# The last 64 keys of two pairs of heads as one unit of four 64x64 tiles, and a new order of all instructions

## The chip, the cores and the metric

One core of one Trainium2 chip runs the whole program. The metric is the device time of one execution in microseconds. The kernel before takes 428.75 us, the median of 3 runs (428.47 to 429.63).

## What is computed

Three layers follow each other: an attention with capped scores over 2 x 12 heads of 448 positions, a gated layer with a mixing matrix over positions (named `moe`), and a mixer layer (`moe2`). Cut to what matters:

```python
def _attn_ref(q, k, v, cap):                     # q, k, v: 2 x 12 x 448 x 64
    scores = q @ k.transpose(0, 1, 3, 2) / np.sqrt(64)
    scores = cap * np.tanh(scores / cap)
    attn = np.exp(scores - np.max(scores, axis=-1, keepdims=True))
    return attn / (np.sum(attn, axis=-1, keepdims=True) + 1e-09) @ v

def _moe_ref(x, w_in, g_ln, w_sg, b_sg, w_out):  # x: 2 x 448 x 768
    u, v = np.split(gelu_tanh(x @ w_in), 2, axis=-1)
    v_s = np.einsum('ts,bsd->btd', w_sg, layer_norm(v) * g_ln) + b_sg[None, :, None]
    return x + (u * v_s) @ w_out

def _moe2_ref(x, w_tok1, w_tok2, w_ch1, w_ch2):
    u = x + (np.maximum(x.transpose(0, 2, 1) @ w_tok1, 0.0) @ w_tok2).transpose(0, 2, 1)
    return u + np.maximum(u @ w_ch1, 0.0) @ w_ch2
```

## The kernel before

Two heads form a pair, 128 partitions wide; there are 12 pairs, 6 for each of the two batches. The 448 keys of a pair are cut into three chunks of 128 and a rest of 64. All matmuls of the attention are in float32, which the trace shows as two records a matmul.

- *Scores* (`scores`, line 578). For a chunk, each head's 64-row block of keys and queries makes one 64x128 tile of TensorE; the two heads run side by side by rows (mode `ROWS`) into a tile `sc` of two PSUM banks, [128 keys, head, 448 queries]. The rest (`last` in `attention_all`, line 692) is done for both heads at once with 128 rows and two column tiles (mode `COLS`); its keys are padded with zeros, and the result [64 keys of head 0 above 64 keys of head 1, 448] goes to one bank of the pool `gm`.
- *Weighing* (`weigh`, lines 554 and 562). ScalarE makes tanh and then exp of each score tile, 896 columns wide for a chunk, 448 for the rest.
- *Values* (`values`, line 591). Four units a pair, one for each chunk and one for the rest, two column tiles side by side (`COLS`), summed up in one bank.
- *Sums* (`sums`, lines 605 and 626). The sums of the weights are a matmul with ones. VectorE or GpSimd adds the chunks first. `LEVEL` says how many tiles are left to separate matmuls: 1 for the first six pairs (the rest has a unit of its own), 0 for the last six (the rest is added too, in two adds of half the partitions).
- *Normalising* (`normalise`): VectorE transposes the sums, takes the reciprocal, transposes back, multiplies the values' bank, and splits the result in a high and a low part for the dense layers.

The dense layers use three matmuls in a reduced float format for one exact one (`three`, line 314). While the second batch's pairs go through the attention, the first batch's seven units of the gated layer (three `v_unit`, four `u_unit`, 18 matmuls each) are put between them; their gelu (line 794) runs after the attention's exps, since it is in another function table of ScalarE. Weights arrive as pairs of 32-bit words and are rebuilt by ScalarE (lines 450, 461, 474) and VectorE.

The order of everything is made by a planner at build time (`Plan.schedule`). Every step is an operation with a duration, a key and buffers from pools of fixed size (`sc` 2, `gm` 4, `a` 21). The planner takes, engine by engine, the operation that can start first, ties by key, with a price for a change of TensorE's mode (`TURN`, `STAY`) and a latency from one engine to the next (`LAT`). The result is a fixed list for each engine, which runs it in that order and waits on semaphores.

## Time and profile before

| What | us |
|---|---|
| median of 3 runs | 428.75 |
| the profiled execution | 427.77 |
| its span, first to last instruction | 425.9 |
| TensorE busy | 415.3 |
| VectorE busy | 253.8 |
| ScalarE busy | 248.9 |

The span is what the trace covers; the profiled execution's own time is 1.87 us longer. PE is TensorE, PEld its weight loads, DVE VectorE, ACT ScalarE, POOL GpSimd. Line numbers are those of the listing above. The attention runs from about 4 to 136 us; its last sums unit starts at 134.96, and the dense stage alone follows from 136.02. The records of TensorE overlap, so the time that a step takes of the engine is the interval between starts.

### The profile page before, as it was taken

The page shows a single profiled execution, that of the slowest core. Times are in us where ns is not written, and L with a number is a line of the kernel's source. Part 1 is how long each engine was busy: PE and PEld are TensorE (multiplying, and loading weights), DVE is VectorE, ACT ScalarE, POOL GpSimd, SP SyncE. Part 2 cuts the span into 40 slices and gives each one's busy share as a digit, 9 for nine tenths or more (in the row PEclk, how much of TensorE's full clock was granted, in tenths as well). Part 3 has the DMA queues.
Part 4 walks back from the last instruction along what each step waited for, and adds up shares of the span by engine and source line. Part 5 has one row for each costly group of instructions (what it writes and reads, how often), then busy time and mean ns, then how long its engine had stood idle before and what let it go on. Part 6 is the DMA issues. An engine that isn't in the chain of part 4 may idle for free. (4 is left out here: it accounts for less than half of the span.)

```text
span 425.9 us, 5397 instructions
## 1 busy us (share of the span) xinstructions
PE 415.3 (98%) x2036; PEld 318.9 (75%) x2036; DVE 253.8 (60%) x407; ACT 248.9 (58%) x372; POOL 89.4 (21%) x88
## 2 busy tenths in 40 slices
PE   8999999999997999999999999999999999999995
PEld 4333335565644899999999989989898899899885
DVE  1859979798645875995556898666312241434211
ACT  6898899889796556426647826575604323444100
POOL 1113130202000321756005295101010010011010
PEclk9999999999998999999999999999999999999999
DMA  7855243442200003005303105544401315442201
GB/s 251 344 164 190 78 169 125 145 163 76 98 1 25 26 10 122 11 2 159 133 0 100 49 3 160 153 131 152 145 0 49 100 45 173 142 148 98 90 21 49
DMA packets 14867, 43.66 MB, mean 102 GB/s; under 512 B 1905, under 2 KB 3569, under 8 KB 14833
## 3 DMA queue, kind: packets, MB, share of 16 engines
q1 hardware_dynamic: 14688, 43.13, 31.2%
q8 instruction: 18, 0.29, 0.3%
q14 instruction: 17, 0.13, 0.1%
q10 hardware_dynamic: 144, 0.10, 0.1%
HBM read 40.47 MB, written 2.75 MB: 101 GB/s over the span
## 5 line engine op out<-in xcount | busy, mean ns | idle before, releaser
L314 PE MATMUL gm<-a,a 128*128 128x384 f32 (+2 forms) x556 | 112.9, 359 | 0.0
L314 PEld LDWEIGHTS gm<-a,a 128*128 128x128 f32 x556 | 100.6, 188 | 8.5
L314 PE MATMUL sc<-x,a 128*128 128x512 f32 (+1 forms) x432 | 87.3, 363 | 0.0
L314 PEld LDWEIGHTS sc<-x,a 128*128 128x128 f32 x432 | 78.3, 188 | 9.0
L481 DVE SCALAR_TENSOR_TENSOR t<-r,t 128x512 int32<-128x512 int32 (+1 forms) x52 | 41.1, 793 | 28.4 <-ACT t L474 27.8
L314 PE MATMUL gm<-q,a 128*128 128x448 f32 (+2 forms) x268 | 57.0, 366 | 0.0
L450 ACT ACTIVATE r<-r 128x512 f32<-128x512 f32 (+1 forms) x58 | 38.9, 670 | 29.2 <-DMA r<-ch_in 27.1
L461 ACT ACTIVATE t<-r 128x512 uint16<-128x512 uint16 (+1 forms) x52 | 40.8, 784 | 24.5 <-DVE a L418 24.2
L314 PEld LDWEIGHTS gm<-q,a 128*128 128x128 f32 x268 | 49.8, 188 | 4.9
L419 POOL TENSOR_TENSOR a<-t,a 128x512 fp32r<-128x512 f32 x17 | 25.8, 1519 | 95.6 <-DVE a L402 65.8
L474 ACT ACTIVATE t<-r 128x512 f16<-128x512 f32 (+1 forms) x52 | 40.3, 775 | 0.0
L418 DVE TENSOR_TENSOR a<-t,a 128x512 fp32r<-128x512 f32 x39 | 27.1, 698 | 20.3 <-POOL a L406 18.8
L406 POOL TENSOR_SCALAR a<-t 128x512 fp32r<-128x512 f32 x18 | 11.2, 619 | 126.7 <-PE gm L314 65.6
L605 DVE TENSOR_TENSOR a<-a,a 128x896 f32<-128x896 f32 x23 | 24.9, 1084 | 20.9 <-ACT a L562 20.8
L591 PE MATMUL gm<-a,v 128*64 128x448 f32 x144 | 33.7, 561 | 3.6 <-ACT a L562 3.6
L554 ACT ACTIVATE a<-sc,qs 128x896 f32<-128x896 f32 x36 | 34.8, 1001 | 3.0 <-PE sc L578 2.9
L562 ACT ACTIVATE a<-a,acap 128x896 f32<-128x896 f32 x36 | 36.2, 1042 | 0.0
L314 PEld LDWEIGHTS gm<-x,a 128*128 128x128 f32 x144 | 26.6, 188 | 6.0 <-issue 2.7
L314 PE MATMUL gm<-x,a 128*128 128x448 f32 x144 | 30.9, 370 | 0.0
L578 PE MATMUL sc<-q 64*128 64x448 f32 x132 | 29.8, 566 | 1.1 <-ACT a L554 0.7
L979 DVE SCALAR_TENSOR_TENSOR a<-sc,a 128x896 fp32r<-128x896 f32 x9 | 9.8, 1091 | 30.4 <-ACT a L976 30.4
L314 PE MATMUL gm<-a,x 128*128 128x512 f32 x108 | 27.2, 406 | 0.0
(102 smaller groups left out, 422.2 us busy)
## 6 DMA issues: line engine op xcount, KB each, us to landing
r<-ch_in SPq DMA_DIRECT2D x36, 512.0 KB, 3.7
r<-w_in_in SPq DMA_DIRECT2D x12, 512.0 KB, 4.8
q<-qk_in SPq DMA_DIRECT2D x11, 480.0 KB, 5.6
v<-va_in SPq DMA_DIRECT2D x12, 256.0 KB, 3.0
r<-w_out_in SPq DMA_DIRECT2D x6, 512.0 KB, 3.1
out_t<-h SPq DMA_DIRECT2D x6, 256.0 KB, 2.3
r<-tok_in SPq DMA_DIRECT2D x2, 512.0 KB, 3.3
out_t<-h SPq DMA_DIRECT2D x5, 192.0 KB, 3.9
```

Of the source, the lines that this page charges most:

```text
L314: self.nc.tensor.matmul(view(), l, rr, start=(i + m == 0), stop=(i + m == n - 1))
L418: "DVE": ("DVE", n / 0.96 + 155, lambda: nc.vector.tensor_tensor(**args()), not psum),
L419: "POOL": ("POOL", n * 2.3 + 60, lambda: nc.gpsimd.tensor_tensor(**args()), True),
L450: lambda: nc.scalar.activation(raw[:, :, 1].bitcast(F32), raw[:, :, 1].bitcast(F32), AF.Copy, scale=2.0**-112),
L461: lambda: nc.scalar.activation(t.ap.bitcast(U16)[:, 0::2], raw.ap.rearrange("p n t -> p (n t)").bitcast(U16)[:, 1::4], AF.Copy, scale=2.0* ...
L474: lambda: nc.scalar.activation(t.ap.bitcast(F16)[:, 1::2], raw[:, :, 1].bitcast(F32), AF.Copy),
L481: lambda: nc.vector.scalar_tensor_tensor(out=t.ap, in0=raw[:, :, 1], scalar=3, in1=t.ap, op0=ALU.logical_shift_left, op1=ALU.bitwise_or),
L554: lambda: nc.scalar.activation(te.ap, sc.ap.rearrange("p (n c) -> p n c", c=512)[:, 0:nn, :S] if nn == 1 else sc[:, 0:nn, :S], AF.Tanh, sc ...
L562: lambda: nc.scalar.activation(te.ap, te.ap, AF.Exp, scale=self.acap),
L578: nc.tensor.matmul(sc[:, h, :S], part(rows, ks), part(rows, QC), start=True, stop=True)
L591: nc.tensor.matmul(A[cols, :S], V[:, 2 * j + h], E[j][:, 0 if j == 3 else h], start=(j == 0), stop=(j == 2),)
L605: "DVE": ("DVE", n / 0.96 + 155, lambda: nc.vector.tensor_tensor(**args()), True),
```

## The change

The last 64 keys of an even pair and the odd pair after it become one unit. `scores_rest` writes one two-bank tile: the even pair's 64 keys in the lower 64 partitions, the odd pair's in the upper, head 0 in one bank and head 1 in the other, by four matmuls of 64 rows and 64 columns (mode `QUAD`). One tanh and one exp of 896 columns follow, and `values_rest` adds both pairs' parts by four 64x64 tiles to the two pairs' banks. The scores of a chunk are cut into 64x64 tiles too (`SPLIT`), four instead of two. `LEVEL` is 0 for all pairs, and the rest is added to a pair's sums in one add of 64 partitions and 896 columns. The zero padding of the keys is gone (`QKW` 960 to 896), and a pair's rest of v lies in the lower or upper partitions by turns.

The planner's durations are new: latency by engine, fixed costs of operations, a price for a change of ScalarE's table, a DMA issue of 420 ns instead of 60. A gelu now waits for all exps of the latest pair. So the order differs everywhere.

```diff
-LEVEL = (1,) * 6 + (0,) * 6
+LEVEL = (0,) * 12
...
-LAT = 140.0
-TURN, STAY = 110.0, 250.0
+LAT = {"PE": 225.0, "ACT": 160.0, "DVE": 140.0, "POOL": 140.0, "SP": 55.0}
+TURN, STAY = 200.0, 250.0
+TABLE = 1290.0
...
+                    if o.table and o.table != table:
+                        c = (max(t, near) + TABLE,) + c[1:3] + (max(t, clock[eng]) + TABLE, o, way)
...
-            ks = slice(KJ[j], KJ[j] + 128)
-            for h, rows in enumerate((LO, UP)):
-                nc.tensor.matmul(sc[:, h, :S], part(rows, ks), part(rows, QC), start=True, stop=True)
-
-        self.pe(3.7, fn, tiles if j else tiles[:1], [sc], key).mode = ROWS
+            for c0 in range(0, 128, 64) if SPLIT else (None,):
+                for h, rows in enumerate((LO, UP)):
+                    at = slice(0, 128) if c0 is None else slice(c0, c0 + 64)
+                    ks = slice(KJ[j] + at.start, KJ[j] + at.stop)
+                    nc.tensor.matmul(sc[at, h, :S], part(rows, ks), part(rows, QC), start=True, stop=True)
+
+        self.pe(3.7, fn, tiles if j else tiles[:1], [sc], key).mode = QUAD if SPLIT else ROWS
...
+    def scores_rest(self, qks, key):
...
+            for (part, _, _), cols in zip(qks, (LO, UP)):
+                for h, rows in enumerate((LO, UP)):
+                    nc.tensor.matmul(sc[cols, h, :S], part(rows, KR), part(rows, QC), start=True, stop=True)
...
+    def values_rest(self, qks, E, As, key):
...
+            for m, rows in enumerate((LO, UP)):
+                for h, cols in enumerate((LO, UP)):
+                    nc.tensor.matmul(As[m][cols, :S], qks[m][2][rows, 6 + h], E[rows, h], start=(m == 1), stop=(m == 0))
...
         if level < 1:
-            for h, rows in enumerate((LO, UP)):
-                f = lambda h=h, rows=rows: F[rows, h]
-                self.add(S, f, f, lambda rows=rows: E[3][rows, 0], [E[3], F], [F], key - 5, ON["F"])
+            rows = (LO, UP)[int(odd)]
+            f = lambda: F[rows]
+            self.add(2 * S, f, f, lambda: E[3][rows], [E[3], F], [F], key - 5, ON["F"])
...
-                self.pe(3.7, last, qk[1], [sc], k0 + 1.3).mode = COLS
-                self.weigh(sc, 1, E[3], k0 + 1.3)
+                if not odd:
+                    sc = self.scores_rest(qks, k0 + KQ)
+                    self.weigh(sc, 2, Q, k0 + KQ)
...
-                self.values(oqk, oE, oA[0], [3, 2], k0 + 2)
-                self.sums(oE, oA[1], k0 + 2.5, LEVEL[n - 1])
+                self.values(oqk, oE, oA[0], [2], k0 + 2, was)
+                if not was:
+                    self.values_rest(oqks, oE[3], oAs, k0 + 2.1)
+                self.sums(oE, oA[1], k0 + 2.5, LEVEL[n - 1], was)
...
-        if self.last_exp:
-
-            o.deps.append(self.last_exp)
+        if self.exps:
+            o.deps += self.exps[max(self.exps)]
```

Three places show what the new order does. A row is a line of the code, the operation, the tile it writes and those it reads, and its shape; `x2` to `x4` are equal instructions in a row. The number behind a tile's name only tells tiles apart. In the new code line 595 is `scores`, 608 `scores_rest`, 621 `values`, 638 `values_rest`, 667 the sums, 323 the dense matmuls, 566 and 575 tanh and exp, 834 gelu.

The first place is TensorE around the value unit of the third chunk of the seventh pair, whose weights are `a_526` before and `a_536` now, up to the first dense matmuls. Before:

```order
L578 MATMUL sc_513<-q_123 128x448 x2
L626 MATMUL gm_449<-a_429,ones 64x448 x2
L591 MATMUL gm_458<-a_493,v_323 64x448 x2
L626 MATMUL gm_497<-a_511,ones 64x448 x2
L591 MATMUL gm_539<-a_503,v_376 64x448 x2
L591 MATMUL gm_539<-a_522,v_376 64x448 x2
L692 MATMUL gm_553<-q_250 64x448 x2
L591 MATMUL gm_539<-h_483,v_376 64x448 x2
L591 MATMUL gm_539<-a_526,v_376 64x448 x2
L578 MATMUL sc_572<-q_250 128x448 x2
L578 MATMUL sc_582<-q_250 128x448 x2
L314 MATMUL gm_589<-a_193,x_230 128x512 x3
```

Now:

```order
L608 MATMUL sc_527<-q_210 64x448 x2
L595 MATMUL sc_542<-q_210 64x448 x4
L595 MATMUL sc_550<-q_210 64x448 x4
L667 MATMUL gm_558<-a_464,ones 64x448 x2
L621 MATMUL gm_562<-a_507,v_390 64x448 x2
L621 MATMUL gm_562<-a_516,v_390 64x448 x2
L621 MATMUL gm_562<-a_536,v_390 64x448 x2
L595 MATMUL sc_585<-q_210 64x448 x4
L595 MATMUL sc_594<-q_278 64x448 x4
L667 MATMUL gm_602<-a_547,ones 64x448 x2
L595 MATMUL sc_611<-q_278 64x448 x4
L323 MATMUL gm_619<-a_214,x_268 128x512 x3
```

Before, the rest of a pair has units of its own here (`L692`, scores of the eighth pair; `L591` with `h_483`, values of the seventh), and the dense matmuls (`L314`) begin three rows behind `a_526`. Now the two rows `L608` are the joint rest of both pairs (the second of them is shown), no value unit of a rest stands here, and the dense matmuls begin five rows behind `a_536`.

The second place is ScalarE at the end of the attention. Before:

```order
L554 ACTIVATE a_1045<-sc_1031,qs 128x896
L554 ACTIVATE a_1055<-sc_1039,qs 128x896
L562 ACT_TABLE_LOAD
L562 ACTIVATE a_1045<-a_1045,acap 128x896
L562 ACTIVATE a_1055<-a_1055,acap 128x896
L554 ACTIVATE a_1073<-sc_1061,qs 128x896
L794 ACT_TABLE_LOAD
L794 ACTIVATE h_964<-h_964 128x448
L562 ACT_TABLE_LOAD
L562 ACTIVATE a_1073<-a_1073,acap 128x896
L794 ACT_TABLE_LOAD
L794 ACTIVATE h_1007<-h_1007 128x448
```

Now:

```order
L566 ACTIVATE a_1071<-sc_1056,qs 128x896
L566 ACTIVATE a_1079<-sc_1063,qs 128x896
L575 ACTIVATE a_1071<-a_1071,acap 128x896
L575 ACTIVATE a_1079<-a_1079,acap 128x896
L566 ACTIVATE a_1106<-sc_1081,qs 128x896
L575 ACTIVATE a_1106<-a_1106,acap 128x896
L410 COPY h_1120<-gm_1090 128x448
L834 ACT_TABLE_LOAD
L834 ACTIVATE h_1127<-a_721 128x512
L834 ACTIVATE h_1134<-a_758 128x512
L834 ACTIVATE h_1137<-a_844 128x512
L834 ACTIVATE h_923<-h_923 128x448
```

Before, three table loads stand between tanh, exp and gelu of the last pair. Now the last exp (`a_1106`) comes first, then one table load, then the gelus in a row.

The third place is TensorE at the same time, up to the last sums (`gm_1114` before, `gm_1131` now). Before:

```order
L578 MATMUL sc_1061<-q_490 128x448 x2
L314 MATMUL gm_1048<-x_411,a_696 128x448 x3
L314 MATMUL gm_1048<-x_477,a_720 128x448 x3
L314 MATMUL gm_1048<-x_570,a_777 128x448 x3
L314 MATMUL gm_1048<-x_577,a_820 128x448 x3
L591 MATMUL gm_1085<-a_1045,v_880 64x448 x2
L591 MATMUL gm_1085<-a_1055,v_880 64x448 x2
L591 MATMUL gm_1085<-h_1019,v_880 64x448 x2
L591 MATMUL gm_1085<-a_1073,v_880 64x448 x2
L314 MATMUL gm_1103<-a_193,x_230 128x512 x3
L314 MATMUL gm_1103<-a_244,x_325 128x512 x3
L626 MATMUL gm_1114<-a_1075,ones 64x448 x2
```

Now:

```order
L595 MATMUL sc_1081<-q_462 64x448 x4
L323 MATMUL gm_1090<-x_268,a_654 128x448 x3
L323 MATMUL gm_1090<-x_362,a_691 128x448 x3
L323 MATMUL gm_1090<-x_423,a_748 128x448 x3
L323 MATMUL gm_1090<-x_511,a_771 128x448 x3
L323 MATMUL gm_1090<-x_609,a_834 128x448 x3
L323 MATMUL gm_1090<-x_674,a_864 128x448 x3
L621 MATMUL gm_1074<-a_1071,v_876 64x448 x2
L621 MATMUL gm_1074<-a_1079,v_876 64x448 x2
L621 MATMUL gm_1074<-a_1106,v_876 64x448 x2
L667 MATMUL gm_1131<-a_1108,ones 64x448 x2
L323 MATMUL gm_1139<-a_214,x_268 128x512 x3
```

Before, six dense matmuls of the next stage (`gm_1103`) stand ahead of the last sums, and a value unit of the rest (`h_1019`) among the last values. Now the whole dense unit `gm_1090` stands between the last scores and the last values, and the next stage (`gm_1139`) begins behind the sums.

## Rows read from the trace of the kernel before

**Rows 1.** The page's busy times: us (share of the span) and instructions of each engine.
```profile
PE 415.3 (98%) x2036; PEld 318.9 (75%) x2036; DVE 253.8 (60%) x407; ACT 248.9 (58%) x372; POOL 89.4 (21%) x88
```

**Rows 2.** Stretches: their us, then busy us of each engine, PEclk, DMA share, GB/s.
```profile
4.00:63.00 59.00, 57.39 (x276) 19.27 (x276) 43.93 (x79) 52.39 (x68) 12.68 (x8) 1.00 0.60 206
63.00:127.00 64.00, 63.61 (x300) 35.57 (x298) 49.96 (x90) 57.21 (x80) 7.04 (x7) 1.00 0.31 101
...
130.90:134.50 3.60, 3.60 (x9) 1.82 (x10) 2.42 (x4) 2.83 (x5) 0.00 (x0) 0.53 0.02 5
...
140.00:400.00 260.00, 260.00 (x1309) 235.98 (x1308) 147.87 (x217) 129.73 (x214) 66.03 (x60) 1.00 0.28 88
```

**Rows 3.** Timeline of TensorE: start us, us to the group's end, what, how many records.
```profile
76.04 4.42 PE L314 MATMUL gm<-a,x 128*128 128x512 f32 x18
80.38 1.77 PE L578 MATMUL sc<-q 64*128 64x448 f32 x8
...
102.34 0.92 PE L591 MATMUL gm<-a,v 128*64 128x448 f32 x4
103.09 0.92 PE L626 MATMUL gm<-a,ones 128*64 128x448 f32 x4
103.94 3.91 PE L314 MATMUL gm<-x,a 128*128 128x448 f32 x18
107.78 1.77 PE L578 MATMUL sc<-q 64*128 64x448 f32 x8
109.49 3.91 PE L314 MATMUL gm<-x,a 128*128 128x448 f32 x18
```

**Rows 4.** Timeline of TensorE at the attention's end.
```profile
130.88 1.71 PE L591 MATMUL gm<-a,v 128*64 128x448 f32 x4 [3.26 <-ACT a L562]
132.53 2.51 PE L314 MATMUL gm<-a,x 128*128 128x512 f32 x6
134.96 1.13 PE L626 MATMUL gm<-a,ones 128*64 128x448 f32 x4
136.02 11.17 PE L314 MATMUL gm<-a,x 128*128 128x512 f32 x48
```

**Rows 5.** Timeline of ScalarE at the attention's end.
```profile
128.50 1.28 ACT L562 ACT_TABLE_LOAD   x1
129.79 1.04 ACT L562 ACTIVATE a<-a,acap 128x896 f32<-128x896 f32 x1
```

**Rows 6.** Timeline of ScalarE in the attention's first part.
```profile
5.73 1.90 ACT L554 ACTIVATE a<-sc,qs 128x896 f32<-128x896 f32 x2 [0.18 <-DVE guard L357]
...
22.47 1.89 ACT L554 ACTIVATE a<-sc,qs 128x896 f32<-128x896 f32 x2
24.25 1.97 ACT L562 ACTIVATE a<-a,acap 128x896 f32<-128x896 f32 x2
26.11 1.90 ACT L554 ACTIVATE a<-sc,qs 128x896 f32<-128x896 f32 x2
...
29.76 0.69 ACT L450 ACTIVATE r<-r 128x512 f32<-128x512 f32 x1
30.34 0.99 ACT L554 ACTIVATE a<-sc,qs 128x896 f32<-128x896 f32 x1
```

**Rows 7.** Waits of ScalarE, 0 to 64 us: us in total, times, longest.
```profile
ACT h L554 <- PE gm L692: 3.7, 2, 2.0
...
ACT a L554 <- PE sc L578: 1.3, 1, 1.3
```

**Rows 8.** Timeline of TensorE at the attention's start.
```profile
3.90 1.39 PE L578 MATMUL sc<-a 64*128 64x448 f32 x4
...
8.29 1.02 PE L578 MATMUL sc<-q 64*128 64x448 f32 x4 [0.39 <-DMA q<-qk_in]
```

**Rows 9.** A group of VectorE on the page: busy us, mean ns, idle before.
```profile
L605 DVE TENSOR_TENSOR a<-a,a 128x896 f32<-128x896 f32 x23 | 24.9, 1084 | 20.9 <-ACT a L562 20.8
```

**Rows 10.** Timeline of TensorE's weight loads among column-tiled units.
```profile
100.08 0.14 PEld L591 LDWEIGHTS gm<-a,v 128*64 128x64 f32 x2 [0.23 <-issue]
```

More of the change, by code (lines that the diff above doesn't have):

```diff
@@ L109 @@
 class Op:
-    __slots__ = ("ways", "key", "seq", "deps", "bufs", "new", "eng", "fn", "start", "end", "nbytes", "nwait", "mode")
+    __slots__ = ("ways", "key", "seq", "deps", "bufs", "new", "eng", "fn", "start", "end", "nbytes", "nwait", "mode", "table")
 class Plan:
@@ L122, in op @@
         o.ways, o.key, o.seq, o.nbytes = ways, key, len(self.ops), nbytes
-        o.deps, o.new, o.mode = [], [], WHOLE
+        o.deps, o.new, o.mode, o.table = [], [], WHOLE, None
         o.bufs = list(dict.fromkeys(list(r) + list(w)))
@@ L180, in schedule @@
         mode = WHOLE
+        table = "exp"
         def earliest(o, way):
@@ L223, in schedule @@
                 mode = o.mode
+            table = o.table or table
             o.eng, dur, o.fn = way[:3]
@@ L241, in schedule @@
                 b.users -= 1
-                b.end = max(b.end, o.end)
+                b.end = max(b.end, o.end + LAT[o.eng])
                 if b.users == 0 and b.tag in free:
@@ L400, in cast @@
         made = {
-            "ACT": ("ACT", n / 1.2 + 180, lambda: nc.scalar.copy(out(), src()), False),
-            "DVE": ("DVE", n / 0.96 / (1 if psum else 2) + 155, lambda: nc.vector.tensor_copy(out(), src()), not psum),
+            "ACT": ("ACT", n / 1.2 + (60 if psum else 95), lambda: nc.scalar.copy(out(), src()), False),
+            "DVE": ("DVE", n / 0.96 / (1 if psum else 2) + 70, lambda: nc.vector.tensor_copy(out(), src()), not psum),
             "POOL": (
@@ L454, in weight @@
                 [raw],
+                130,
                 key=key,
@@ L553, in weigh @@
             nn * S,
-            lambda: nc.scalar.activation(te.ap, sc.ap.rearrange("p (n c) -> p n c", c=512)[:, 0:nn, :S] if nn == 1 else sc[:, 0:nn, :S], AF.Tanh, scale=self.qs),
+            lambda: nc.scalar.activation(te.ap, sc[:, 0:nn, :S], AF.Tanh, scale=self.qs),
             [sc, self.cb],
             [te],
-            60,
+            145,
             key,
+            "exp",
         )
-        self.last_exp = self.exps[int(key // 10)] = self.act(
+        e = self.act(
             nn * S,
@@ L564, in weigh @@
             [te],
-            190,
+            185,
             key + dt,
+            "exp",
         )
+        self.exps.setdefault(int(key // 10), []).append(e)
     def scores(self, qk, j, key):
@@ L593, in av, with fn @@
                         V[:, 2 * j + h],
-                        E[j][:, 0 if j == 3 else h],
-                        start=(j == 0),
-                        stop=(j == 2),
+                        E[j][:, h],
+                        start=(j == 0 and not odd),
+                        stop=(j == 2 and odd),
                     )
             self.pe(3.7, av, [V, E[j]], [A], key).mode = COLS
+    def values_rest(self, qks, E, As, key):
+        nc = self.nc
+        def fn():
+            for m, rows in enumerate((LO, UP)):
+                for h, cols in enumerate((LO, UP)):
+                    nc.tensor.matmul(As[m][cols, :S], qks[m][2][rows, 6 + h], E[rows, h], start=(m == 1), stop=(m == 0))
+        self.pe(3.7, fn, [qks[0][2], qks[1][2], E], As, key).mode = QUAD
     def add(self, n, out, a, b, r, w, key, on):
@@ L608, in add, with sums @@
         self.plan.op([made[e] + (t,) for e, t in on.items()], key, r, w)
-    def sums(self, E, A, key, level):
+    def sums(self, E, A, key, level, odd):
         nc = self.nc
@@ L676, in attention_all @@
             k0 = 10.0 * n
+            odd = n % 2 == 1
             if n < B * NP:
-                qk = self.pair_in(n)
+                if not odd:
+                    qks = [self.pair_in(n), self.pair_in(n + 1)]
+                    Q = self.a([128, 2, S])
+                    As = [self.bank(), self.bank()]
+                qk = qks[odd]
                 E = {j: self.a([128, 2, S]) for j in range(3)}
-                E[3] = self.h([128, 1, S])
-                A = [self.bank() for _ in range(2)]
+                E[3] = Q
+                A = [As[odd], self.bank()]
                 for j in range(3):
@@ L684, in attention_all @@
                     self.weigh(sc, 2, E[j], k0 + 0.4 * j)
[L685 to L700 removed]
+                if not odd:
+                    sc = self.scores_rest(qks, k0 + KQ)
+                    self.weigh(sc, 2, Q, k0 + KQ)
+            if old:
+                was = odd == 0
+                oqk, oE, oA, oqks, oAs = old
+                self.values(oqk, oE, oA[0], [0, 1], k0 - 2, was)
+                self.values(oqk, oE, oA[0], [2], k0 + 2, was)
+                if not was:
+                    self.values_rest(oqks, oE[3], oAs, k0 + 2.1)
+                self.sums(oE, oA[1], k0 + 2.5, LEVEL[n - 1], was)
                 xs.append(self.normalise(n - 1, oA))
             if n < B * NP:
[L703 removed]
+                old = qk, E, A, qks, As
         return xs
@@ L793, in gelu @@
     def gelu(self, out, src, n):
-        o = self.act(n, lambda: self.nc.scalar.activation(out.ap, src[:, :n], AF.Gelu_apprx_tanh), [src], [out], 100)
-        if self.last_exp:
-            o.deps.append(self.last_exp)
+        o = self.act(n, lambda: self.nc.scalar.activation(out.ap, src[:, :n], AF.Gelu_apprx_tanh), [src], [out], 85, table="gelu")
+        if self.exps:
+            o.deps += self.exps[max(self.exps)]
     def pack(self, x):
@@ L1209, in layout @@
             va[:, :, :, 2 * j + h] = vp[:, :, h, j * 128 : (j + 1) * 128]
-        qk[:, :, h, :, KJ[3] + 64 * h : KJ[3] + 64 * h + 64] = kh[..., REST]
+        qk[:, :, h, :, KR] = kh[..., REST]
         qk[:, :, h, :, QC] = q.reshape(B, NP, 2, S, D)[:, :, h].transpose(0, 1, 3, 2)
-        va[:, :, 64 * h : 64 * h + 64, 6 + h] = vp[:, :, h, REST]
+        for p in range(NP):
+            va[:, p, (LO, UP)[p % 2], 6 + h] = vp[:, p, h, REST]
     return {
```

61 lines of the change are left out of this document (31 added, 30 removed).

## The prediction

> **What bounds the kernel now.** The page's first part comes first: TensorE is busy 98% of the span, no other engine more than 60% [rows 1]. A busy share is a mean over stages, so the table of stretches is read next [rows 2]. From 140 to 400 us TensorE is busy for all 260 us: that part is its own work alone, and this change adds and removes nothing there. The change lies in the attention, from 4 to about 136 us. Up to 63 us TensorE is busy 57.4 of 59 us and ScalarE 52.4: nearly level. From 63 to 127 us it is 63.6 of 64 against 57.2.
>
> The timeline of TensorE gives the prices there [rows 3]. I call a unit one score, value or sum step of a pair of heads (two matmuls side by side, four records). The interval from one unit's start to the next is the price, not the record's length, since records overlap: 102.34 to 103.09, 0.75 us. A change of tiling costs a little more: 103.09 to 103.94 is a unit and a change, so 0.10; 107.78 to 109.49 is two score units and a change, so 0.21. A dense unit of 18 matmuls with the change behind it takes 4.34 us at 512 columns (76.04 to 80.38) and 3.84 at 448 (103.94 to 107.78).
>
> At the end of the attention stands the one long wait [rows 4]: TensorE is idle for 3.26 us before 130.88, for an exp of ScalarE. The timeline of ScalarE shows why [rows 5]: between the last tanh and its exp it runs a gelu, which needs another table, and so loads exp's table once more (128.50, 1.28 us) before the exp at 129.79. Behind the wait the granted clock was 0.53 for 3.6 us, near the lower level of 1.2 GHz [rows 2]. What stands from 130.88 to 136.02 (5.14 us) would at full clock be a unit with its change (0.95), six matmuls and a change (6 x 0.23 + 0.1) and a unit with a change (0.85), 3.3 us; the clock cost about 1.8. The stall is worth 5.0 us in all.
>
> **The change part by part.** (1) Units removed. For two pairs of heads, 2 last-key score units become 1 and 2 last-key value units become 1: over six such couples 6 + 6 units. The sums of the first six pairs lose the separate last-key unit: 6 more. 18 x 0.75 = 13.5 us of TensorE's time.
>
> (2) Score units in four 64x64 tiles. 36 score units, 6 joint score units and 6 joint value units are now eight records instead of four. The trace has no unit of four tiles. Below: 0.75 us, if all four run side by side, with nothing to gain, since rows-tiled and column-tiled units already cost the same 0.75. Above: 1.5 us, if only two run at once. I take 0.75: both nearest rows run as many tiles at once as fit, two by rows at 107.78 and two by columns at 102.34 [rows 3].
>
> (3) ScalarE's order at the end. In the new order all 42 tanh and 42 exp stand ahead of the one table load for gelu. The 5.0 us go. Late next there would be the last exp and two adds of VectorE behind it; TensorE has 18 dense matmuls (3.84 us) and three value units (2.3 us) between the last score unit and the last sums, against tanh, exp and two adds (0.89 + 0.93 + 2 x 1.08 = 4.0 us, behind at most 1.8 us of exps): covered.
>
> (4) ScalarE becomes the limit of the first part. I follow the new order to the third exp of the seventh pair (tile a_536), ahead of any dense unit. On ScalarE 25 tanh, 24 exp and 6 weight scalings come first. A tanh takes 0.89 us from start to start, an exp 0.93, a scaling 0.58 [rows 6]: 22.3 + 22.3 + 3.5 = 48.1 us. From the first tanh at 5.73 that ends at 53.8. TensorE needs less to get there: from its first score unit at 3.90 [rows 8], 55 units (41.4 us) and 26 changes at 0.2 give 50.5. So TensorE waits there. ScalarE itself is held up at times: before, it was idle 5.0 us up to 64 us because TensorE fed it late [rows 7]. Now TensorE is ahead, and I put 1.5 us. With 0.2 for the handover (exp at 129.79 plus 0.93, unit at 130.88) the value unit of a_536 starts at 55.5.
>
> (5) From there TensorE sets the time. Up to the last sums there are 41 units (30.8 us), 3 dense units at 4.34 (13.0) and 4 at 3.84 (15.4), and 13 more changes at 0.2 (2.6): 61.8. With 0.5 of waits (0.4 in 63 to 127 us before) the sums end at 117.8, against 136.0. Before, six dense matmuls of the next stage were done by then (6 x 0.23 = 1.4), now none: the gain is 18.2 - 1.4 = 16.8 us.
>
> (6) Costs put at nothing. TensorE's joint score unit of the first couple needs the second pair's keys, which landed near 8.3 us [rows 8]; TensorE comes there about 7 and waits a microsecond, hidden since ScalarE reaches that tile only at 10.3. If ScalarE were the faster, it would cost 1. Sums now add the last keys on VectorE in all twelve pairs: 36 full-width adds instead of 23 there and one on GpSimd, less seven of half the width: 13 x 1.08 less about 4 [rows 9], 10 us more on an engine that was busy 94 of the 123 us. Its work up to the last sums is then about 104 of 114 us: covered, with little left. After the attention the seven postponed gelus run in one row; their users on VectorE stand behind the last pair's transposes in both orders, and TensorE has some 31 us of dense units before it reads them.
>
> Sum: span 425.9 - 16.8 = 409.1. The profiled execution took 427.77, 1.87 beside its span: 411.0. The median of 428.75 lies 0.98 above it: **412.0 us**. As a check, 13.5 + 5.0 taken off whole would give 410.3; the difference is the first part, where removed units only turn into waiting for ScalarE.
>
> **The rivals.** *Two tiles at a time* (slower). If four tiles share what two had, a four-tile unit takes 1.5 us. 30 of the 48 lie before a_536: TensorE gets there at 50.5 + 30 x 0.75 = 73 instead of 55.5, and the other 18 add 13.5. That is 31 us: 443. It decides from the point where 48 units, less the 5 us that TensorE has to spare, eat the 16.8: about 0.45 us more per unit. Against it: both kinds of two-tile unit hide everything but their columns. For it: no row shows eight records in 0.75 us.
>
> *Weight loads no longer hidden* (420). In a four-tile unit two tiles share the same 64 rows. If each tile pair's load of 0.14 us then stood in the open, twice a unit, 18 units add 4.9 us behind a_536, and 30 units make TensorE late there by 50.5 + 8.2 - 55.5 = 3.2: 8.1 us more. Against it: column-tiled units load 64 columns at 100.08 while matmuls on the same 128 rows run, and keep 0.75 us [rows 10]. The Trainium skill, TensorE: Matmul & The Clock Gate, section The mechanism, says that weight loads overlap running matmuls only where the row group differs; by that rule the loads would be in the open and 420 would come out. This trace disagrees with the rule for column tiles, so I give it little.
>
> *Handovers* (418 to 419). Three engines are nearly full at once. If ScalarE is held up for 5.0 us in the first part as before, that is 3.5 more, and if each of the last six sums waits half a microsecond for VectorE's second and third add, 3 more. For it: VectorE has about 10 us to spare; against it: nearly no such wait in 63 to 127 us.
>
> *The stall moves.* If the order's end leaves a wait of some 3 us and another drop of the clock (5.0 us), 417. The table loads are gone from that place, so only a late add could cause it.
>
> **How the numbers follow.** Forecast, 407 to 415: 0.64. Handovers or a moved stall, 415 to 420: 0.15. Loads in the open, 418 to 423: 0.09. Two at a time or near it: 0.07. Better than 407 (no hold-up of ScalarE, changes at 0.1, and the waits gone together are 3.3 us: 408.7): 0.05. The forecast's own range is 407 to 415; 8 in 10 needs 406 to 420. A measurement of this kernel tells 0.3% (1.3 us) from no change. All cases but two-at-a-time end more than that below 428.75; with a little for what I did not think of: faster 0.90, same 0.03, slower 0.07.
>
> **What would show it.** Right: score units of eight records 0.75 us apart; one table load for gelu, behind the last exp; no wait over 2 us and no fall of the clock before 125 us; the last sums near 118 us; short waits of TensorE for ScalarE before 56 us and few behind. Wrong: four-tile units at 1.0 us or more, or tiles starting in two pairs; ScalarE idle over 4 us up to a_536; a wait for VectorE's adds at the sums; TensorE idle anywhere behind 120 us, where I count on none.

## The result and the profile after

The changed kernel takes 414.64 us, the median of 4 runs (414.54 to 414.90), against 429.07 for the kernel before on the same chip (428.47 to 429.63, 4 runs): a ratio of 0.9665, 95% interval 0.9648 to 0.9682. In a later comparison it was 415.54 (414.45 to 415.61, 5 runs) against 428.49, a ratio of 0.9689 (0.9675 to 0.9703). The forecast was 412.0 in a range of 406 to 420, faster. The profiled execution took 414.54 with a span of 412.8; the sum had put the span at 409.1. So 3.7 us have to be found. The medians lie only 2.6 us apart, because the sum's last two terms came out smaller: the profiled execution was 1.74 us longer than its span (1.87 before), and the median lies 0.10 above it (0.98 before).

The page's busy times of the changed kernel, us and share of the span, answer to [rows 1]:

```profile
PE 401.0 (97%) x2156; PEld 309.5 (75%) x2156; DVE 260.4 (63%) x417; ACT 239.8 (58%) x352; POOL 79.9 (19%) x82
```

TensorE has 14.3 us less to do, VectorE 6.6 more. The stretches, with the columns of [rows 2]:

```profile
4.00:63.00 59.00, 54.42 (x378) 15.53 (x379) 51.37 (x86) 55.95 (x66) 12.88 (x9) 1.00 0.58 202
...
120.00:140.00 20.00, 20.00 (x92) 16.98 (x91) 16.79 (x39) 12.18 (x23) 6.60 (x8) 1.00 0.08 26
140.00:400.00 260.00, 258.74 (x1307) 234.66 (x1305) 140.76 (x200) 119.49 (x195) 55.42 (x50) 1.00 0.27 90
```

Three things are to be seen. Up to 63 us TensorE is now busy 54.4 of 59 us, behind ScalarE's 55.95, with VectorE at 51.4 (it was 43.9): the first part has gone over to the other two engines. A narrower stretch says it more plainly: from 22.7 to 59.4 us ScalarE is busy all the time and VectorE 36.2 of 36.7 us (in the kernel before 33.4 and 29.1):

```profile
22.70:59.40 36.70, 33.19 (x236) 9.25 (x232) 36.16 (x58) 36.70 (x43) 11.28 (x8) 1.00 0.46 152
```

The attention's end has no wait and no fall of the clock any more: 20.00 of 20 us at 1.00. And from 140 to 400 us, where TensorE had been busy for all 260, 1.26 us are missing, in a stage that the change does not edit.

TensorE's waits over the whole run name the engines (us in total, times, longest):

```profile
PE sc L595 <- ACT a L566: 2.2, 3, 1.1
PE gm L667 <- DVE a L646: 2.1, 3, 1.0
PE sc L323 <- DVE x L427: 1.3, 2, 0.7
```

L595 are the scores and L566 the tanh, L667 the sums and L646 VectorE's adds for them. The third line is the one in the dense part: L323 are the first channel product's matmuls, L427 VectorE's splits of x in a high and a low part.

The timeline of TensorE among the four-tile units answers to [rows 3], and the end of the attention to [rows 4]:

```profile
51.79 1.88 PE L595 MATMUL sc<-q 64*64 64x448 f32 x16 [1.12 <-ACT a L566]
...
54.40 2.42 PE L621 MATMUL gm<-a,v 128*64 128x448 f32 x12
...
59.47 0.97 PE L667 MATMUL gm<-a,ones 128*64 128x448 f32 x4 [0.98 <-DVE a L646]
...
61.56 3.01 PE L323 MATMUL gm<-a,x 128*128 128x512 f32 x12 [0.21 <-DVE h L702]
...
65.84 0.98 PE L595 MATMUL sc<-q 64*64 64x448 f32 x8 [0.35 <-ACT a L566]
...
84.78 1.73 PE L595 MATMUL sc<-q 64*64 64x448 f32 x16
86.33 0.93 PE L638 MATMUL gm<-a,v 64*64 64x448 f32 x8
87.08 1.71 PE L595 MATMUL sc<-q 64*64 64x448 f32 x16
88.72 0.47 PE L323 MATMUL gm<-x,a 128*128 128x448 f32 x1
...
118.36 0.92 PE L667 MATMUL gm<-a,ones 128*64 128x448 f32 x4
119.21 3.02 PE L323 MATMUL gm<-a,x 128*128 128x512 f32 x12
```

The joint value unit, eight records, lasts from 86.33 to 87.08, 0.75 us; two score units before it take 1.55, two behind it with a change of tiling 1.64. The group at 54.40 holds three value units, the third of them a_536's, which so starts near 55.9, without a wait of its own.

To see in which stage each kernel gains or loses, I read from TensorE's timeline when each stage begins. "Next stage" is the first matmul of the gated layer's mixed unit behind the attention's own dense units, "ch1" and "ch2" the two channel products of the last layer; times in us of the profiled execution.

| kernel | next stage | ch1 | ch2 | ch1 lasts | span |
|---|---|---|---|---|---|
| before | 147.03 | 247.50 | 334.67 | 87.17 | 425.9 |
| changed | 131.59 | 232.10 | 321.28 | 89.18 | 412.8 |
| changed, second profile (e9) | 132.35 | 232.87 | 322.05 | 89.18 | 413.8 |
| e1 | 133.24 | 233.85 | 323.04 | 89.19 | 414.7 |
| e2 | 141.31 | 241.92 | 329.09 | 87.17 | 420.2 |
| e3 | 140.89 | 241.50 | 330.59 | 89.09 | 421.9 |
| e4 | 134.64 | 235.25 | 322.42 | 87.17 | 414.0 |
| e5 | 132.22 | 232.74 | 319.94 | 87.20 | 411.9 |
| e6 | 133.41 | 234.02 | 323.10 | 89.08 | 414.7 |
| e10 | 131.90 | 232.42 | 319.62 | 87.20 | 411.6 |

The column of the next stage holds a scatter of the start. The two profiles of the changed kernel differ in it by 0.76 us, and 0.70 of this is there at the first tanh (5.32 and 6.02 us), which waits for a small constant to land. Behind it ScalarE has no idle time up to the exp at 53.38 (54.06 in the second profile), so a late start is carried along. The first tanh starts at 5.73 in the kernel before, at 5.81 in e2, 5.91 in e3, 6.41 in e4 and 5.84 in e6, so differences below about 1 us in this column say little.

So the 3.7 us are 1.4 in the attention (147.03 - 131.59 = 15.4 gained, 16.8 forecast), 2.0 at ch1 (89.18 - 87.17), and 0.3 between the end of TensorE's last matmul (421.63 before, 408.24 now) and the end of the span (4.27 us, now 4.56). The middle (131.59 to 232.10) is the 100.5 us that it was.

### The profile page after: what moved, and what is told of

Read it like the earlier page. It is cut to its first block, busy times and chain, and to the rows that moved or that the text cites. A ratio compares the mean times of both kernels' runs of the same rounds, so it can differ in the third digit from the quotient of the medians.

```text
span 412.8 us, 5606 instructions
## 1 busy us (share of the span) xinstructions
PE 401.0 (97%) x2156; PEld 309.5 (75%) x2156; DVE 260.4 (63%) x417; ACT 239.8 (58%) x352; POOL 79.9 (19%) x82
## 5 line engine op out<-in xcount | busy, mean ns | idle before, releaser
L323 PE MATMUL gm<-a,a 128*128 128x384 f32 (+2 forms) x556 | 112.9, 359 | 0.0
L323 PEld LDWEIGHTS gm<-a,a 128*128 128x128 f32 x556 | 100.6, 188 | 8.5
L323 PE MATMUL sc<-x,a 128*128 128x512 f32 (+1 forms) x432 | 88.1, 364 | 1.3 <-DVE x L427 1.3
L323 PEld LDWEIGHTS sc<-x,a 128*128 128x128 f32 x432 | 78.1, 188 | 11.2 <-DVE x L427 2.1
L493 DVE SCALAR_TENSOR_TENSOR t<-r,t 128x512 int32<-128x512 int32 (+1 forms) x52 | 40.3, 777 | 27.1 <-ACT t L485 26.9
L459 ACT ACTIVATE r<-r 128x512 f32<-128x512 f32 (+1 forms) x58 | 39.0, 672 | 31.7 <-DMA r<-ch_in 26.4
L323 PE MATMUL gm<-q,a 128*128 128x448 f32 (+2 forms) x268 | 57.0, 366 | 0.0
L323 PEld LDWEIGHTS gm<-q,a 128*128 128x128 f32 x268 | 49.8, 188 | 4.9
L646 DVE TENSOR_TENSOR a<-a,a 128x896 f32<-128x896 f32 (+1 forms) x36 | 40.7, 1137 | 8.9 <-ACT a L575 8.4
L427 DVE TENSOR_TENSOR a<-t,a 128x512 fp32r<-128x512 f32 x44 | 33.7, 768 | 19.9 <-POOL a L415 18.8
L575 ACT ACTIVATE a<-a,acap 128x896 f32<-128x896 f32 x42 | 42.3, 1060 | 0.0
L566 ACT ACTIVATE a<-sc,qs 128x896 f32<-128x896 f32 x42 | 40.7, 1024 | 2.2 <-PE sc L595 1.9
L428 POOL TENSOR_TENSOR a<-t,a 128x512 fp32r<-128x512 f32 x12 | 20.1, 1678 | 91.6 <-ACT r L459 42.3
L595 PE MATMUL sc<-q 64*64 64x448 f32 x264 | 30.3, 553 | 1.5 <-ACT a L566 1.5
L621 PE MATMUL gm<-a,v 128*64 128x448 f32 x144 | 31.1, 548 | 0.4 <-ACT a L575 0.4
L323 PE MATMUL gm<-x,a 128*128 128x448 f32 x144 | 30.5, 368 | 0.0
L323 PEld LDWEIGHTS gm<-x,a 128*128 128x128 f32 x144 | 26.7, 188 | 4.9 <-issue 1.4
L1015 ACT ACTIVATE a<-sc 128x896 fp32r<-128x896 f32 x9 | 8.3, 922 | 32.4 <-PE sc L323 32.4
```

The source lines that it names most:

```text
L323: self.nc.tensor.matmul(view(), l, rr, start=(i + m == 0), stop=(i + m == n - 1))
L427: "DVE": ("DVE", n / 0.96 + 70, lambda: nc.vector.tensor_tensor(**args()), not psum),
L428: "POOL": ("POOL", n * 2.3 + 60, lambda: nc.gpsimd.tensor_tensor(**args()), True),
L459: lambda: nc.scalar.activation(raw[:, :, 1].bitcast(F32), raw[:, :, 1].bitcast(F32), AF.Copy, scale=2.0**-112),
L493: lambda: nc.vector.scalar_tensor_tensor(out=t.ap, in0=raw[:, :, 1], scalar=3, in1=t.ap, op0=ALU.logical_shift_left, op1=ALU.bitwise_or),
L566: lambda: nc.scalar.activation(te.ap, sc[:, 0:nn, :S], AF.Tanh, scale=self.qs),
```

## The experiments

**The parts one by one.** The first four separate units, tiles, order and stall.

*e1, a chunk's scores in two tiles again*, in the order of the changed kernel:

```diff
-            for c0 in range(0, 128, 64) if SPLIT else (None,):
+            for c0 in (None,):
```

> The changed kernel, its order untouched, but each chunk's scores in two tiles of 64x128 again; only the joint rest stays in four 64x64 tiles. If a unit of four tiles costs what a unit of two costs (0.75 us), only changes of tiling differ: six joint score units now stand between units of another tiling, and six joint value units beside them, up to 12 more changes at 0.1 to 0.2 us: 414.6 to 417. If four tiles cost more than two (1.0 us a unit), this kernel is the faster one by 36 x 0.25 = 9 us, about 406. If four tiles are themselves a gain, it loses more than 3 us.

Measured 416.67 (416.39 to 416.85), a ratio to before of 0.9723 (0.9699 to 0.9747): 2.0 us more than the changed kernel. The units in its trace, TensorE's timeline:

```profile
85.37 1.77 PE L595 MATMUL sc<-q 64*128 64x448 f32 x8
87.07 0.98 PE L638 MATMUL gm<-a,v 64*64 64x448 f32 x8
87.99 1.77 PE L595 MATMUL sc<-q 64*128 64x448 f32 x8
```

Score units of two 64x128 tiles cost the same, but each neighbour of another tiling now costs a change: 1.70 instead of 1.55 for the two units up to the joint value unit, 0.92 instead of 0.75 for that one. In the whole attention TensorE changes its tiling 61 times in e1's trace and 46 times in the changed kernel's. At 0.10 (from [rows 3]) to 0.17 us (these rows) 15 changes are, as an estimate, 1.5 to 2.6 us; the next stage begins 1.65 us later. The chunk's cut into four tiles gains by the changes it spares, not by the unit.

*e2, only the stall of the kernel before taken away*: gelu waits for all exps of the last pair instead of the one made last.

```diff
-            o.deps.append(self.last_exp)
+            o.deps += self.lasts[max(self.lasts)]
```

> The kernel before with one edit: a gelu waits for every exp of the last pair, not only for that of its rest. If the stall at the attention's end was the two extra changes of ScalarE's table (my 5.0 us: 3.26 of waiting and 1.8 of half clock), this takes 424. If TensorE would have waited there for the last exp anyway, or the seven gelus in a row now hold up the next stage, 427 to 429.

Measured 422.35 (422.03 to 422.62), ratio 0.9857 (0.9833 to 0.9882), 6.3 us less than the 428.61 beside it. The next stage began 5.7 us sooner. TensorE at the attention's end:

```profile
127.29 0.92 PE L593 MATMUL gm<-a,v 128*64 128x448 f32 x4
128.04 0.92 PE L628 MATMUL gm<-a,ones 128*64 128x448 f32 x4
128.89 7.36 PE L315 MATMUL gm<-a,x 128*128 128x512 f32 x31
```

Neither the 3.26 us of [rows 4] nor the slow clock of [rows 2] is left. The stall was worth 5.7 us, somewhat more than the 5.0 of the forecast, and it stands by itself: 5.7 of the 15.4 us gained in the attention are the place of the gelus alone. The kernel before loads a function table five times from 117 us on, for gelu and exp by turns (the text ahead of the prediction speaks of three); e2 and the changed kernel load one there, for gelu, behind the last exp.

*e3, the units of before with all the new planner numbers*, and *e4, the new units with the old numbers*. Among the numbers that were exchanged, old above new:

```diff
-LAT = 140.0
-TURN, STAY = 110.0, 250.0
+LAT = {"PE": 225.0, "ACT": 160.0, "DVE": 140.0, "POOL": 140.0, "SP": 55.0}
+TURN, STAY = 200.0, 250.0
+TABLE = 1290.0
...
```

> The units of the kernel before (a rest for each pair, LEVEL 1 for six pairs, two tiles) with all the planner's new numbers, the price of a table change and the new wait of gelu. My theory: the stall goes (5.0) and the small waits may shrink by 1: 423 to 424, and the wait of TensorE at the first channel units (2 us) may come with the new numbers: then 425. The rival, that the new order and not the removed units bring most of the 14 us: 418 or less.

> The joint units, four tiles and LEVEL 0 of the changed kernel with all the planner's old numbers and the old rule for gelu (it waits for the exp created last, now that of a whole chunk, so one table load is left here too). My theory: 18 units and the stall are gone, 414 to 418, with the small waits differing by 1 or 2 us from the changed kernel. The rival, that the joint units only pay with the new numbers: 420 or more.

Measured: e3 423.57 (423.04 to 423.95), ratio 0.9882 (0.9856 to 0.9908); e4 416.77 (415.92 to 416.89), ratio 0.9726 (0.9703 to 0.975). The ch1 column of the table is what they are worth: e3 shows the lost 2 us, e4 and e2 do not. The loss comes with the planner's new numbers, with the old units as well, and not with the units. The column of the next stage says what the new units are worth in the attention under the new numbers: from e3 to the changed kernel the next stage begins 9.3 us sooner (up to 0.6 of it can be the start), where 18 units at 0.75 are 13.5 us and the forecast, 16.8 less 5.0 for the stall, left 11.8 for them. The new numbers do help there: the next stage begins 3.05 us sooner in the changed kernel than in e4, about 2 when the later start of e4 is taken off, and TensorE's waits in e4 (L584 are its scores, L557 its tanh) show what the old numbers leave:

```profile
PE sc L584 <- ACT a L557: 4.8, 5, 1.8
```

That is ScalarE again, as the limit of the first part.

**The 2 us at ch1.** In the changed kernel TensorE waits twice there. Its timeline, VectorE's and GpSimd's:

```profile
232.10 4.51 PE L323 MATMUL sc<-x,a 128*128 128x512 f32 x19
237.21 0.96 PE L323 MATMUL sc<-x,a 128*128 128x512 f32 x3 [0.59 <-DVE x L427]
238.84 8.38 PE L323 MATMUL sc<-x,a 128*128 128x512 f32 x42 [0.67 <-DVE x L427]
```

```profile
229.18 1.27 DVE L1052 TENSOR_TENSOR h<-gm,h 128x448 f32<-128x448 f32 x2
230.37 3.73 DVE L427 TENSOR_TENSOR x<-h,x 128x448 fp32r<-128x448 f32 x3
234.02 1.14 DVE L1052 TENSOR_TENSOR h<-gm,h 128x448 f32<-128x448 f32 x2
235.09 0.71 DVE L493 SCALAR_TENSOR_TENSOR t<-r,t 128x512 int32<-128x512 int32 x1
235.72 3.06 DVE L427 TENSOR_TENSOR x<-h,x 128x448 fp32r<-128x448 f32 x2
```

```profile
230.60 1.67 POOL L428 TENSOR_TENSOR a<-t,a 128x512 fp32r<-128x512 f32 x1
232.22 14.69 POOL L1098 TENSOR_TENSOR h<-x 128x384 f32<-128x384 f32 x10
```

Three splits take 3.73 us and two 3.06, where such a split has a median of 0.62 us; two of L1052 between them, which read PSUM, take 1.14 together, as elsewhere. Beside the slow ones GpSimd runs without a break: but for one subtraction (L428) it adds the two halves of x (L1098), which only ch2 wants, from 321 us on. By single records each of the five splits that are slow here started while an instruction of GpSimd was running, and ended 0.48 us behind that instruction's end. The kernel before had the same neighbours and slow splits as well (VectorE's timeline of before):

```profile
245.76 2.98 DVE L418 TENSOR_TENSOR x<-h,x 128x448 fp32r<-128x448 f32 x3
```

But in its order TensorE had 24 matmuls on the four splits already there, twelve each for two outputs, before it wanted the last two; the new order has twelve and six. So there were two suspects: GpSimd, or the orders. *e5* holds GpSimd's adds back by a copy of 64 columns from the first channel unit's result, ahead of the first add:

```diff
-                self.gps(
-                    size // n * 2.3 + 60,
-                    lambda o=o[i], parts=parts: nc.gpsimd.tensor_tensor(out=o.ap, in0=parts(0), in1=parts(1), op=ALU.add),
-                    [U[0][d], U[1][d]],
-                    [o[i]],
-                )
+                def add(o=o[i], parts=parts, first=(m, d) == (0, 0)):
+                    if first:
+                        nc.gpsimd.tensor_copy(o.ap[:, 0:64], h2[0][1].ap.bitcast(F32)[:, 0:64])
+                    nc.gpsimd.tensor_tensor(out=o.ap, in0=parts(0), in1=parts(1), op=ALU.add)
+                self.gps(size // n * 2.3 + 60, add, [U[0][d], U[1][d], h2[0][1]], [o[i]])
```

> The changed kernel, with GpSimd's twelve adds of the two halves of x (wanted only at the very end, by the second channel product) held back until the first channel unit's result is there. Theory: these adds run beside VectorE's last split adds (1.24 and 1.53 us each instead of 0.6) and so cause the 2.0 us lost at the start of the channel units; then the split adds come back to 0.6 to 0.9 us, TensorE's two waits there (0.59 and 0.67 us) go, and the time falls by 1.2 to 2.2 us, to 412.4 to 413.4. Rival: the loss is the order of TensorE (two products of four splits and of two before the last two splits are wanted, where the kernel before had four and four) and VectorE's order; then the waits stay within 0.3 us of what they were and the time stays at 414.3 to 415. Point that decides: the duration of the split adds between 229 and 239 us, and TensorE's idle time there.

Measured 413.31 (412.69 to 413.75), ratio 0.9646 (0.9634 to 0.9659). TensorE's order at the start of ch1 is unchanged, twelve and six. Its timeline, then VectorE's and GpSimd's:

```profile
232.74 17.46 PE L323 MATMUL sc<-x,a 128*128 128x512 f32 x84
```

```profile
232.24 1.69 DVE L427 TENSOR_TENSOR x<-h,x 128x448 fp32r<-128x448 f32 x3
233.84 0.61 DVE L1052 TENSOR_TENSOR h<-gm,h 128x448 f32<-128x448 f32 x1
234.38 0.68 DVE L493 SCALAR_TENSOR_TENSOR t<-r,t 128x512 int32<-128x512 int32 x1
235.09 0.43 DVE L411 CAST a<-t 128x512 fp32r<-128x512 f32 x1
235.43 0.62 DVE L427 TENSOR_TENSOR x<-h,x 128x448 fp32r<-128x448 f32 x1
```

```profile
230.36 1.75 POOL L428 TENSOR_TENSOR a<-t,a 128x512 fp32r<-128x512 f32 x1 [1.55 <-ACT a L410]
...
244.00 4.16 POOL L1099 TENSOR_TENSOR h<-x 128x512 f32<-128x512 f32 x3
```

The three splits take 1.69 us instead of 3.73, the last one 0.62; both waits of TensorE are gone, and ch1 lasts 87.20 us, as before. VectorE's order moved by a place or two with it (one split stands ahead of L493 now, and L411 ahead of the last one), so the edit is not of GpSimd alone; but a changed order could end the waits, and would not bring each split back to its 0.61 us. GpSimd's adds are the cause of the 2 us; the short order makes them count, as the kernel before shows, which had the slow splits and no wait.

**The 1.4 us in the attention.** *e6* gives the first six pairs their sums unit for the fourth key tile back:

```diff
-LEVEL = (0,) * 12
+LEVEL = (1,) * 6 + (0,) * 6
```

> The changed kernel with VectorE's adds of the fourth key tile left out in the first six pairs, and a sums unit of TensorE of its own for it instead: six units more, 6 x 0.75 = 4.5 us. Theory: the first part of attention waits for ScalarE and VectorE (of TensorE's waits in it 2.1 us were for VectorE's sums and 2.2 for ScalarE), so that much of the 4.5 lands in these waits: plus 1.5 to 2.8 us, 416.1 to 417.4, with VectorE's waits of the sums gone. Rival: the adds cost nothing, as the prediction put them; then TensorE's six units come on top in full: plus 4.2 to 4.8, 418.8 to 419.4.

Measured 416.75 (416.44 to 417.42), ratio 0.9731 (0.9718 to 0.9743), 2.1 us over the 414.64 of the changed kernel and 1.2 over its later 415.54; by the traces the next stage begins 1.8 us later (up to 0.5 of it can be the start). Six units are 4.5 us of TensorE, so the larger part came back as waits that went: TensorE's idle time in the attention fell from 4.93 to 2.27 us. TensorE's waits over the whole run in e6, then VectorE's adds from 4 to 63 us, in e6 and in the changed kernel:

```profile
PE sc L595 <- ACT a L566: 1.3, 1, 1.3
...
PE gm L667 <- DVE a L646: 0.3, 1, 0.3
```

```profile
L646 DVE TENSOR_TENSOR a<-a,a 128x896 f32<-128x896 f32 (+1 forms) x15 | 16.4, 1098 | 7.2 <-ACT a L575 7.2
```

```profile
L646 DVE TENSOR_TENSOR a<-a,a 128x896 f32<-128x896 f32 (+1 forms) x21 | 24.6, 1180 | 5.7 <-ACT a L575 5.4
```

The waits for the adds fall from 2.1 to 0.3 us. The six sums units that the change moved to VectorE in the first part are worth 1.8 us by these traces and 1 to 3 by the medians and ratios, not 4.5.

The mean of an add is 1.18 us in the changed kernel and 1.10 in e6. Behind this stand two adds of 2.16 and 2.17 us, at 22.74 and 38.63, which started while a subtraction of GpSimd (L428) was running. The other way round, the three adds at 53.66 kept their 1.07 us, and the subtraction that started beside them took 3.99 us instead of 1.27. VectorE's and GpSimd's timelines of the changed kernel:

```profile
38.63 2.17 DVE L646 TENSOR_TENSOR a<-a,a 128x896 f32<-128x896 f32 x1
...
53.66 3.08 DVE L646 TENSOR_TENSOR a<-a,a 128x896 f32<-128x896 f32 x3
```

```profile
38.59 1.27 POOL L428 TENSOR_TENSOR a<-t,a 128x512 fp32r<-128x512 f32 x1 [2.75 <-DVE a L411]
...
53.91 3.99 POOL L428 TENSOR_TENSOR a<-t,a 128x512 fp32r<-128x512 f32 x1 [4.83 <-DVE a L411]
```

From the first of the two slow adds to the sums unit at 59.47 VectorE has no gap over 0.04 us, so the 2.2 us that the two lost can be the whole of TensorE's three waits for it. No run takes only these meetings with GpSimd away, and e6 changed both, the number of adds and the meetings; so how much of the waits is the six adds, and how much GpSimd, stays open.

*e7* and *e8* try ScalarE's side: the first dense weights are scaled (L459, 0.70 us each) later, out of the way of the exps.

```diff
-    "win_v": (6, 8),
+    "win_v": (50, 4),      # e8: (66, 2)
```

> The changed kernel with the due times of the first dense weights (win_v) from 50 in steps of 4 instead of from 6 in steps of 8: two of ScalarE's scalings (0.70 us each) instead of six stand ahead of the exps of the first 28 units. Theory: ScalarE limits the first part, so the value unit of a_536 (55.9 us) comes some 2 us sooner, and the attention's end by 1 to 2 us, until TensorE's own work limits it: 412.6 to 413.8. Rival: ScalarE's lead is worth nothing, since TensorE has the same work and then lacks dense matmuls to fill its waits with; or the scalings moved behind delay the dense matmuls: 414.3 to 416.

> The same with due times from 66 in steps of 2: no scaling before the thirtieth exp, the dense matmuls come some 18 instructions later in TensorE's order. Theory of ScalarE's limit: as much as with four moved or more, 412 to 413.8, as long as the dense matmuls are not late. Rival: VectorE's conversions of the same weights then come in one lump with the sums' adds, and TensorE has nothing to fill its waits with before: 414.5 to 418.

Both went the rivals' way, and further than I had put it: e7 422.21 (421.03 to 422.44), ratio 0.9845 (0.9831 to 0.9859); e8 431.76 (431.09 to 433.61), ratio 1.0087 (1.0069 to 1.0105), slower than the kernel before. Stretches of e7, then of e8:

```profile
4.00:56.00 52.00, 50.53 (x354) 15.00 (x354) 42.19 (x74) 50.46 (x59) 3.27 (x4) 1.00 0.56 188
...
63.00:90.00 27.00, 20.21 (x114) 8.83 (x108) 26.74 (x44) 20.08 (x27) 9.33 (x4) 0.95 0.33 115
```

```profile
4.00:56.00 52.00, 51.70 (x370) 15.61 (x372) 40.59 (x70) 49.91 (x56) 0.30 (x1) 1.00 0.50 168
...
63.00:90.00 27.00, 17.82 (x80) 7.96 (x81) 24.69 (x41) 18.02 (x24) 5.78 (x5) 0.75 0.35 123
```

Half of the theory is borne out: up to 56 us TensorE does 50.5 and 51.7 us of work, against 48.6 in the changed kernel. But from 63 to 90 us it is short by 6.8 and 9.2 us, and waits for the dense weights, which VectorE (26.7 of 27 us busy in e7) and GpSimd now make in one lump; in e8 the granted clock was 0.75 in the mean besides. What ScalarE gives in the first part is taken with interest behind it.

**A version that is better than both.** The last three ran side by side on one chip: the changed kernel, e5's kernel, and e5's with the weights' due times moved a little, `"win_v": (12, 8)`.

> The changed kernel once more, to stand on the same chip as the next two: 414 to 415 us. The profile of its first run and that of the one with the halves added later differed by 0.6 us before 10 us in the program, where both have the same instructions; if that is a scatter of the start, it shows again here in one or the other, and is no part of either kernel.

> GpSimd's adds of the halves held back, beside the changed kernel on one chip. By the trace, where the first channel product takes 87.2 us instead of 89.2: 2.0 us less than the run before this one, 412.3 to 413.3. If the stage's gain were given back later (the second channel product needs the sums, and GpSimd is in its way with them later), 414 or more.

> The same with the due times of the first dense weights from 12 instead of from 6 in unchanged steps of 8: the six scalings of ScalarE stay spread, each some exps later. If ScalarE's order in the first part still has something to give (its two exps behind a scaling come sooner): 0.3 to 1.2 us less than the run before. If the amount of its work is all that counts there, as its 50.9 busy of 52 us say: within 0.4 us of it. If VectorE's waits for the sums grow with it: up to 1 us more.

Measured: e9 415.54 (414.45 to 415.61), ratio 0.9689 (0.9675 to 0.9703); e10 412.56 (412.52 to 413.37), ratio 0.9630 (0.9617 to 0.9643); e11 415.77 (415.23 to 416.05), ratio 0.9700 (0.9686 to 0.9713). With GpSimd's adds held back the kernel is faster than the changed one, without an overlap of the runs; of the 3.0 us between the medians 2.0 are ch1 by the traces (89.18 us in e9, 87.20 in e10), and the rest is no more than the runs of e9 differ among themselves. e11, 3.2 us above e10, fell outside all that I had expected: one sums unit alone waits 2.85 us for VectorE, one of whose adds ahead of it took 2.16 us beside a subtraction of GpSimd.

## Why the prediction was right, and where it was short

*Four-tile units (step 2): right.* 0.75 us for eight records, the lower bound: the first four of them, one for each tile, start within 0.02 us. The rival of two tiles at a time (443) and that of weight loads in the open (420) are both out: in either the units would lie 1.0 us or more apart. The Trainium skill, TensorE: Matmul & The Clock Gate, section The mechanism, has a load hidden only behind a matmul of another row group; the trace disagrees once more, since two of the four tiles share their rows, the last four weight loads of the unit at 86.33 start beside its first four matmuls, and the unit keeps its 0.75 us.

*The stall (step 3): the mechanism right, the size small.* 5.0 forecast, 5.7 by e2's trace. No wait and no slow clock took its place. The sum does not use the size, since it follows the new order from 3.90 us to the last sums.

*ScalarE as the limit of the first part (step 4): right, but the time of a_536 was met by luck.* Its 25 tanh, 24 exp and 6 scalings took the 48.1 us of the sum to the tenth (5.32 to 53.38 us). But of the 1.5 us for which ScalarE was to be held up none came, and it started 0.4 us sooner than before, so by the sum's own terms the value unit could have started at 53.6; even the exp behind that one had ended at 54.5. It started at 55.9, with no wait before it. TensorE had waited earlier, 1.12 us up to 51.79, for the tanh that ended at 51.74 and so left a score tile free; from there it had five units to do before a_536's. So ScalarE holds TensorE through the two score tiles and not through the exp, and a hold-up too large and a path too short gave 55.5 together. The sum's own work of TensorE up to there was short as well: 48.6 us without the waits, where 46.6 stood. e4 and e7 show the limit from two sides.

*The way from there (step 5): the work right, the waits mis-sized.* The work from a_536 to the end of the last sums was 61.8 us, as forecast. I put 0.5 us of waits; the rows above show 0.98, 0.21 and 0.35, together 1.54. With the 0.4 of step 4 this is the 1.4 us that the attention missed. Most of it is the wait of a sums unit for VectorE.

*Costs put at nothing (step 6): the term of the attention that was too small.* "10 us more on an engine that was busy 94 of the 123 us ... covered, with little left" is a statement on a sum over the attention. From 22.7 to 59.4 us VectorE was full, and the sums units waited for it 0.33 and 0.78 us up to a_536 and 0.98 behind it, where step 5 had 0.5 us for all waits. e6 shows that these waits go when the adds go; the two long meetings with GpSimd go with them there, and which of the two it was stays open. What e6 calls the prediction's case, 4.5 us in full, did not follow from it: five of the six units lie ahead of a_536, where step 4 gave TensorE 5.0 us to spare.

*"TensorE idle anywhere behind 120 us, where I count on none": wrong, and the largest miss, 2.0 us.* I read the stretch of 260 busy us as untouched, since the change edits no operation there. The planner's new numbers reach every stage: they took away six matmuls that had covered slow splits at ch1, and e3 loses the same 2 us with the old units. The trace of before had the slow splits beside GpSimd's adds to show, and the two orders had the six matmuls.

The rival of handovers (418 to 419) named the right kind of loss, waits for VectorE's adds, but put it at the last sums, where there was none, and counted on a ScalarE held up for 5.0 us, which was not held up at all. The case "better than 407" does not reach below 407 by its own working, which gives 408.7.

Two of the prediction's own signs of being wrong came, a wait for VectorE's adds at the sums and an idle TensorE behind 120 us; both were small. So the mechanism was right in the main, and the measured time within the range; that the median is missed by only 2.6 us owes 0.9 to the distance of the median from the profiled execution, which came out at 0.10 and not 0.98.

## What to carry to other kernels

When a planner's numbers change, every stage is edited: look in the stages that are "TensorE alone" for work on other engines that is covered by only a few matmuls, and compare the order there too. Units taken from a full engine are worth their price only where no other engine is as full in that same stretch; make the sum for each stretch, and not over the stage. And try whether work that is wanted late can be made to wait: an idle engine that runs it early can slow a neighbour that is wanted now, as GpSimd did here for 2.0 us. A time that comes out right is worth following back to what ended just before it: a_536's was right for another reason than the one put down.

## What was not expected of the hardware

- VectorE and GpSimd held each other up where both worked on two operands in SBUF, and the one that had started first kept its pace. VectorE's split, 128x448, has a median of 0.618 us and took up to 1.705 us when it started while an instruction of GpSimd was running; in e5 all twelve were within 0.609 to 0.618 us. One of these started at 230.356, 8 ns ahead of a subtraction of GpSimd, which then took 1.75 us instead of the 1.30 of the next one. VectorE's adds from PSUM in the same place kept 0.61 to 0.63 us apiece.
- The first score units ran at two paces with the same instructions. In the changed kernel's first profile the second pair of units starts at 4.71, in its second one at 5.45, and both start at 3.90; the stretch from 3.90 to 5.40, first profile and second:

```profile
3.90:5.40 1.50, 1.50 (x17) 0.51 (x16) 0.58 (x5) 0.28 (x2) 0.00 (x0) 1.00 0.77 157
```

```profile
3.90:5.40 1.50, 1.50 (x9) 0.55 (x12) 0.03 (x1) 0.00 (x0) 0.00 (x0) 1.00 0.84 239
```

  Seventeen records against nine. The granted clock of 1.00 in both rows does not contradict this: the trace's first record of the clock, at full level, begins at 3.87 us in the first profile and at 5.76 in the second, and the view shows 1.00 for the time ahead of it, too. In the second profile the matmul records that start at 3.90 and 4.70 last 1.01 and 0.95 us, the one at 5.45 0.70 and the one at 5.98 0.54; in the first profile they last 0.59 and 0.54 from the start. In e10 and e5, whose clock records begin at 5.26 and 5.79 us, the first records of 0.54 us start at 5.36 and 6.00. So the slow pace goes with the time that has no record of the full level. Ahead of it TensorE ran the same twelve small matmuls from 1.04 us in both profiles; why the level rose at different times stays open. It is not the scatter between the profiles, which follows the landing of the small constant (VectorE uses it first at 4.68 us in the one and at 5.38 in the other).
